# Top-k attention and two gated layers: the second layer's leaky maximum as one parametric relu, and the rounding pass of its weights on another engine

## The chip, the cores and the metric

The kernel runs on one core of one Trainium2 chip. A core has five engines that run side by side, each with a queue of its own that it works through in order: PE (TensorE, matrix products), DVE (VectorE), ACT (ScalarE), POOL (GpSimd) and SP (SyncE, which here only issues transfers). Sixteen DMA engines move data. The metric is device time in microseconds (us) of one execution; lower is better. Times stand as the median of several runs.

## The reference

Three stages follow one another: attention that keeps the 32 largest scores of each row, a layer with a squared relu, and a layer with a leaky maximum. The change touches only the last.

```python
def _attn_ref(q, k, v):                       # 4 batches, 8 heads, 576 rows, 64 wide
    scores = scale * np.matmul(q, k.transpose(0, 1, 3, 2))
    kth = np.partition(scores, -top_k, axis=-1)[..., -top_k:-top_k + 1]
    scores = np.where(scores >= kth, scores, -1000000000.0)
    ...
    return np.matmul(attn, v).astype(np.float32)

def _moe_ref(x, w_in, w_out):                 # x 2304 x 512, w_in 512 x 2048, w_out 2048 x 512
    h = np.maximum(x @ w_in, 0.0)
    return (h * h @ w_out).astype(np.float32)

def _moe2_ref(x, w_in, w_out):
    h = x @ w_in
    g = np.maximum(0.01 * h, h)
    return (g @ w_out).astype(np.float32)
```

## The kernel before, in words

**Precision by splitting.** Products run on numbers rounded to a shorter form. Each operand is therefore kept as two parts: a rounded high part and the remainder. A pass that copies a tile into the rounded form makes the high part, and a subtraction makes the remainder. A product of two split operands is three matmuls: high with high, high with low, low with high.

**Attention.** Scores (L276) are brought out by ACT (L277). DVE then finds the 32 largest of each row with four passes of MAX8 (L828) and three of MATCH_REPLACE8 (L830). ACT masks and exponentiates (L294, a parametric relu; L298), POOL normalizes (L307), PE transposes (L312, L325) and multiplies with the values (L407). The 2304 rows are worked through in 72 pairs of tiles; a "slot" is one sixteenth of a pair, and nearly every step has its slot written in the code.

**The two layers.** The 2304 rows form six blocks of 512, 256, 384, 512, 256 and 384 rows. For each block j and layer there is a phase (j, layer) of 16 steps f, one for each 128 hidden columns. The order of the phases is (0,0) (0,1) (1,0) (1,1) (2,0) (2,1) (3,0) (3,1) (4,0) (5,0) (4,1) (5,1). A step f of `moe` does this:

- 12 matmuls into the PSUM tile `h` (L574), of which there is one buffer (`bufs=1`): the next step's first matmul has to wait until ACT has read it.
- The activation, from `h` into `ga`, then its rounded part `gh` and the remainder `gl` (L600).
- The second product into `acc` for the step before (`LAG = 1`), first with `gh`, then with `gl`: L617 in layer 0, L619 in layer 1. So on PE the order is h(f), acc(f-1), h(f+1), acc(f).

In layer 1 and blocks 0 to 4 the activation is two ACT passes over `h`, one for each sign (L595 into `ga`, L596 into `gb`), and a subtraction on POOL (L597). Then ACT makes `gh` (L599) and POOL `gl`. In block 5 it is an ACT copy scaled by 0.01 (L591) and a maximum on DVE (L592).

**The weights.** They come as 64-bit numbers. In the first phase of each layer, (0,0) and (0,1), `w_convert_steps` turns the two weight tiles of each step (`wi`, `wo`, 128x512) into single precision and splits them: two ACT passes (L508, L509), two DVE passes (L513, L514), one ACT pass for the high part (L518) and a POOL subtraction (L520). It is begun two steps ahead of its use. The result is stored (L528, L529) and loaded again in later phases (L536). `split_hi` is a helper that does the same rounding on ACT (L113) or on POOL (L115), as its third argument says.

**What sets the order.** The pieces of `moe` are emitted between the attention's slots, so many per slot that a group of phases ends about when the next block's rows are ready. A scheduler then sets the order on each engine by priorities and a modelled timeline; at run time each engine's order is fixed.

Of the kernel before, what the change touches and what calls it, by code (L numbers as in the profile page):

```python
# [8 lines left out]
F = mybir.dt.float32  # L9
R = mybir.dt.float32r  # L10
U = mybir.dt.uint32
AF = mybir.ActivationFunctionType
OP = mybir.AluOpType
# [50 lines left out]
KLO_D = ((0, 0), (0, 1))  # L64
QLO_D = (0,)

LEAK2 = 5
GLD = 5


# [1 line left out]
def topk_attention_moe_moe2_kernel(  # L72
# [12 lines left out]
    P = 128  # L85
# [8 lines left out]
    PE, ACT, DVE, POOL, SP = nc.tensor, nc.scalar, nc.vector, nc.gpsimd, nc.sync  # L94
# [6 lines left out]
    def bank():  # L101
        return psum.tile([P, 512], F, tag="att", name="att", bufs=3)
# [4 lines left out]
    def behind(key):  # L107

        return tc.issue_after(cur[key].ins) if key in cur else ExitStack()

    def split_hi(dst, src, act=False):
        if act:
            ACT.activation(dst, src, AF.Copy)  # L113
            return
        POOL.tensor_scalar(dst, src, 1.0, 1.0, op0=OP.mult, op1=OP.mult)  # L115
# [9 lines left out]
    for u in units:  # L125
        for hp in range(NHP):
            n = u["n"]
# [46 lines left out]
    late = {}  # L174
# [197 lines left out]
    def block_x(blk):  # L372

        if "x" not in blk:
            i = SETS[blk["idx"]]
            m = max(x["n"] for x in blocks if SETS[x["idx"]] == i)
            if i == 2:
                ts = [pool.tile([P, 2, m], R, tag="wraw", name="x2", bufs=WRB) for _ in range(NK)]
                blk["x"] = [(t[:, 0], t[:, 1]) for t in ts]
            else:  # L380
                xpool = late["mlp"] if i else pool
                ts = [xpool.tile([P, NK, m], R, tag=f"x{c}{i}", name=f"x{c}{i}", bufs=1) for c in "hl"]
                blk["x"] = [(ts[0][:, c], ts[1][:, c]) for c in range(NK)]
        return blk["x"]
# [76 lines left out]
    steps = [(j, layer, f) for j, layer in phases for f in range(NF)]  # L461
# [8 lines left out]
    def w_alloc(i):  # L470
        wi = pool.tile([P, 2, 512], R, tag="wi", name="wi", bufs=3)
        wo = pool.tile([P, 2, 512], R, tag="wo", name="wo", bufs=4)
        wt[i] = (wi, wo)
        return wi, wo
# [24 lines left out]
    def w_convert_steps(i):  # L499
        if i >= len(steps) or not fresh[i]:  # L500
            return
        w2 = w_alloc(i)
        for raw, w in zip(wraw.pop(i), w2):
            if W64:
                lo, hi = raw[:, :, 0], raw[:, :, 1]
                b = pool.tile([P, 512], U, tag="wc", name="wc", bufs=WCB)
                v = bank()
                ACT.activation(b, lo, AF.Copy, scale=L_SCALE, bias=L_BIAS)  # L508
                ACT.activation(v, hi.bitcast(F), AF.Copy, scale=H_SCALE)  # L509
                yield 0  # L510
                vu, c = v.bitcast(U), b.bitcast(F)
                with behind("dve"):
                    DVE.scalar_tensor_tensor(b, vu, 3, b, op0=OP.logical_shift_left, op1=OP.bitwise_or)  # L513
                DVE.scalar_tensor_tensor(b, vu, 0x80000000, b, op0=OP.bitwise_and, op1=OP.bitwise_or)  # L514
                yield 0
            else:
                c = raw
            ACT.activation(w[:, 0, :], c, AF.Copy)  # L518
            yield 0
            POOL.tensor_tensor(w[:, 1, :], c, w.bitcast(F)[:, 0, :], op=OP.subtract)  # L520
            yield 0
# [30 lines left out]
    def moe(j, layer):  # L552
        blk = blocks[j]
        n = blk["n"]
        x = block_x(blk)
        base = phases.index((j, layer)) * NF
        na = NK if layer == 0 else n // P
        gs = {}
        for f in range(NF + LAG):
            conv = iter(())  # L560
            if f < NF:
                si = base + f
                w_store(si + 1)
                conv = w_convert(si + 2)
                w_load(si + 2)
                wi, wo = wt.pop(si)
                h = late["psum"].tile([P, 512], F, tag="h", name="h", bufs=1)
                cnt = 0
                if f == 0:
                    mm = [(w, c, 0) for w in range(2) for c in range(NK)] + [(0, c, 1) for c in range(NK)]  # L570
                else:
                    mm = [(0, c, y) for c in range(NK) for y in range(2)] + [(1, c, 0) for c in range(NK)]
                for w, c, y in mm:
                    PE.matmul(h[:, 0:n], lhsT=wi[:, w, c * P:(c + 1) * P], rhs=x[c][y][:, 0:n], start=cnt == 0,  # L574
                              stop=cnt == 3 * NK - 1)
                    cnt += 1
                    if cnt % MQ == 0 and cnt < 3 * NK:
                        next(conv, None)
                        yield
                gh = late["mlp"].tile([P, 512], R, tag="gh", name="gh", bufs=2)  # L580
                gl = late["mlp"].tile([P, 512], R, tag="gl", name="gl", bufs=2)
                a = late["mlp"].tile([P, 512], F, tag="ga", name="ga", bufs=2)
                if layer == 0 and j < GLD:
                    ACT.activation(a[:, 0:n], h[:, 0:n], AF.Relu)  # L584
                    ACT.activation(gh[:, 0:n], a[:, 0:n], AF.Square)  # L585
                    POOL.tensor_tensor(a[:, 0:n], a[:, 0:n], a[:, 0:n], op=OP.mult)  # L586
                elif layer == 0:
                    ACT.activation(a[:, 0:n], h[:, 0:n], AF.Relu)
                    ACT.activation(a[:, 0:n], a[:, 0:n], AF.Square)
                elif j >= LEAK2:  # L590
                    ACT.activation(a[:, 0:n], h[:, 0:n], AF.Copy, scale=0.01)  # L591
                    DVE.tensor_tensor(a[:, 0:n], a[:, 0:n], h[:, 0:n], op=OP.max)  # L592
                else:
                    b = late["mlp"].tile([P, 512], F, tag="gb", name="gb", bufs=1)
                    ACT.activation(a[:, 0:n], h[:, 0:n], AF.Relu)  # L595
                    ACT.activation(b[:, 0:n], h[:, 0:n], AF.Relu, scale=-0.01)  # L596
                    POOL.tensor_tensor(a[:, 0:n], a[:, 0:n], b[:, 0:n], op=OP.subtract)  # L597
                if layer or j >= GLD:
                    ACT.activation(gh[:, 0:n], a[:, 0:n], AF.Copy)  # L599
                (DVE if j >= GLD else POOL).tensor_tensor(gl[:, 0:n], a[:, 0:n], gh.bitcast(F)[:, 0:n],  # L600
                                                          op=OP.subtract)
                gs[f] = (gh, gl, wo)
                next(conv, None)
                yield
            if f >= LAG:
                ff = f - LAG
                if ff == 0:
                    acc = [late["psum"].tile([P, 512], F, tag="acc", name="acc", bufs=4) for _ in range(na)]
                gh, gl, wo = gs.pop(ff)
                mm = [(c, w, gh) for c in range(na) for w in range(2)] + [(c, 0, gl) for c in range(na)]  # L610
                if ff == NF - 1:
                    mm.sort(key=lambda m: m[0])
                for i, (c, w, g) in enumerate(mm):
                    cs = slice(c * P, (c + 1) * P)
                    first, last = ff == 0 and g is gh and w == 0, ff == NF - 1 and g is gl
                    if layer == 0:
                        PE.matmul(acc[c][:, 0:n], lhsT=wo[:, w, cs], rhs=g[:, 0:n], start=first, stop=last)  # L617
                    else:
                        PE.matmul(acc[c], lhsT=g[:, cs], rhs=wo[:, w, :], start=first, stop=last)  # L619
                    if i % 3 == 2:  # L620
                        next(conv, None)
                        yield
            for _ in conv:
                pass
            if f < NF:
                w_raw(si + 4)
        for c in range(na):
            if layer == 0:
                xh, xl = x[c]
                ACT.activation(xh[:, 0:n], acc[c][:, 0:n], AF.Copy)  # L630
                DVE.tensor_tensor(xl[:, 0:n], acc[c][:, 0:n], xh.bitcast(F)[:, 0:n], op=OP.subtract)  # L631
            else:
                y = pool.tile([P, 512], F, tag="wc", name="y", bufs=WCB)
                ACT.activation(y, acc[c], AF.Copy)  # L634
                for p0, n0, r0 in rows(blk["g0"] + c * P, P):
                    ACT.dma_start(out[r0:r0 + n0, :], y[p0:p0 + n0])
# [16 lines left out]
    for uh in uhs:  # L653
        b, hp, i = uh["b"], uh["hp"], uh.get("di")
# [158 lines left out]
    while slot <= last:  # L813
        p, i = divmod(slot, 16)
# [89 lines left out]
```

## Time and profile before

| | |
|---|---|
| Median of 3 runs | 1206.67 us (1203.94 to 1209.59) |
| Profiled execution, its own time | 1204.04 us |
| Span of the profiled execution | 1202.3 us |
| Mean granted TensorE clock | 0.979 |
| Busy share of the span: PE, DVE, ACT, POOL | 94%, 79%, 66%, 57% |

The span runs from the first to the last instruction; 1.7 us lie outside it. In the profile the phase (0,0) begins at 173.2 us, (0,1) at 325.4 us, (1,0) at 434.9 us, (4,0) at 963.1 us. These are the starts of the 1st, 193rd, 385th and 1537th matmul of L574. The attention's last MAX8 runs at 962.6 us, so from 963.1 us on the layers are alone.

### The profile page before, as it was taken

What the parts mean: (1) busy time and instruction counts of PE and PEld (TensorE: products, weight loads), DVE (VectorE), ACT (ScalarE), POOL (GpSimd) and SP (SyncE); (2) the same over time, 40 slices, a digit from 0 to 9 for tenths busy, and PEclk for the clock granted to TensorE, in tenths of its full rate; (3) what the DMA queues carried; (4) which work ended last, traced back from release to release, by engine and by line L of the source; (5) the groups of instructions that cost most, each with busy time, mean ns of one, the idle gap of its engine ahead of it and who ended that gap; (6) DMA issues with size and microseconds to landing.
All of it is one profiled execution on the core that took longest, in us unless ns stands there. A gap on an engine that the chain in (4) does not pass through costs nothing.

```text
span 1202.3 us, 20196 instructions
## 1 busy us (share of the span) xinstructions
PE 1133.4 (94%) x6388; PEld 993.1 (83%) x6388; DVE 945.0 (79%) x1944; ACT 798.8 (66%) x1819; POOL 679.4 (57%) x922
## 2 busy tenths in 40 slices
PE   5999967998899999999999999999999999999998
PEld 4777845886677889988998998888788899999997
DVE  7999999768988899999999999999999920110122
ACT  6999978678999986766665666555675653334322
POOL 7967565677889876456665665545456554004200
PEclk9899978898999999999999999999999999999999
DMA  9868556679889888889988888777676689879974
GB/s 302 288 208 264 204 197 210 219 244 347 312 285 339 297 289 289 291 279 398 332 284 294 266 282 289 221 228 225 198 223 225 191 270 374 253 247 351 353 250 137
DMA packets 110522, 323.25 MB, mean 269 GB/s; under 512 B 17488, under 2 KB 25680, under 8 KB 110416
## 3 DMA queue, kind: packets, MB, share of 16 engines
q1 hardware_dynamic: 107776, 317.24, 78.3%
q10 hardware_dynamic: 2640, 4.72, 1.1%
q8 instruction: 52, 0.85, 0.3%
q14 instruction: 54, 0.44, 0.1%
HBM read 254.54 MB, written 67.37 MB: 268 GB/s over the span
## 4 chain that ended last, share of the span: by engine, by line
PE 56%; DVE 4%; ACT 1%; DMA 1%; issue 0%; POOL 0%; SPq 0%; ACTq 0%
PE h L574 24%; PE acc L617 12%; PE acc L619 12%; PE att L407 3%; PE att L312 3%; DVE m L828 2%; DVE w L830 1%; PE att L325 1%; DVE PTs L318 1%; DMA vraw<-in_v_dram 0%; PE att L276 0%; DVE xl L631 0%; ACT y L634 0%; DMA wi<-wd 0%; ACT e L298 0%
## 5 line engine op out<-in xcount | busy, mean ns | idle before, releaser
L574 PE MATMUL h<-xh,wi 128*128 128x512 f32 (+2 forms) x1280 | 349.2, 345 | 14.4 <-ACT gb L596 4.9
L828 DVE MAX8 m<-w 128x8 f32<-128x576 f32 x432 | 312.9, 747 | 1.4
L574 PEld LDWEIGHTS h<-xh,wi 128*128 128x128 f32 x1280 | 227.5, 191 | 41.7 <-ACT gb L596 6.6
L830 DVE MATCH_REPLACE8 w<-m,w 128x576 f32<-128x576 f32 x288 | 213.2, 742 | 0.7
L574 PE MATMUL h<-xl,wi 128*128 128x512 f32 (+2 forms) x640 | 207.3, 342 | 2.3 <-DVE xl L631 1.3
L600 POOL TENSOR_TENSOR gl<-ga,gh 128x512 fp32r<-128x512 f32 (+2 forms) x160 | 163.3, 1021 | 44.6 <-ACT gh L599 40.6
L617 PE MATMUL acc<-gh,wo 128*128 128x512 f32 (+2 forms) x768 | 155.9, 341 | 0.0
L619 PE MATMUL acc<-wo,gh 128*128 128x512 f32 x576 | 152.4, 399 | 1.5 <-ACT gh L599 1.5
L597 POOL TENSOR_TENSOR ga<-ga,gb 128x512 f32<-128x512 f32 (+2 forms) x80 | 81.6, 1020 | 107.9 <-ACT gb L596 106.9
L294 ACT ACTIVATE e<-s,m 128x576 f32<-128x576 f32 x144 | 112.5, 782 | 39.2 <-DVE m L828 32.1
L617 PEld LDWEIGHTS acc<-gh,wo 128*128 128x128 f32 x768 | 126.2, 189 | 10.9 <-ACT gh L585 0.4
L574 PEld LDWEIGHTS h<-xl,wi 128*128 128x128 f32 x640 | 121.2, 191 | 14.8 <-DVE xl L631 3.7
L619 PEld LDWEIGHTS acc<-wo,gh 128*128 128x128 f32 x576 | 103.8, 188 | 21.6 <-ACT gh L599 2.6
L586 POOL TENSOR_TENSOR ga<-ga 128x512 f32<-128x512 f32 (+2 forms) x80 | 66.4, 830 | 84.7 <-ACT gh L585 76.5
L298 ACT ACTIVATE e<-e,nb 128x576 f32<-128x576 f32 x144 | 110.8, 774 | 4.7 <-POOL nb L288 4.4
L828 DVE MAX8 m<-s 128x8 f32<-128x576 f32 x144 | 103.8, 747 | 8.3 <-ACT s L277 5.1
L830 DVE MATCH_REPLACE8 w<-m,s 128x576 f32<-128x576 f32 x144 | 106.9, 743 | 0.4
L312 PE MATMUL att<-ident,e 128*128 128x128 f32 x576 | 88.5, 281 | 18.3 <-ACT e L298 13.9
L584 ACT ACTIVATE ga<-h 128x512 f32<-128x512 f32 (+2 forms) x80 | 39.2, 490 | 85.5 <-PE h L574 77.1
L307 POOL TENSOR_SCALAR e<-e,rc 128x576 f32<-128x576 f32 x108 | 80.0, 753 | 28.2 <-DVE rc L303 26.2
L312 PEld LDWEIGHTS att<-ident,e 128*128 128x128 f32 x576 | 70.2, 144 | 29.9 <-ACT e L298 18.2
L599 ACT ACTIVATE gh<-ga 128x384 fp32r<-128x384 f32 (+2 forms) x112 | 58.4, 522 | 44.7 <-POOL ga L597 34.8
(94 smaller groups left out, 2153.0 us busy)
## 6 DMA issues: line engine op xcount, KB each, us to landing
wi<-wd SPq DMA_DIRECT2D x160, 512.0 KB, 5.0
wo<-wd SPq DMA_DIRECT2D x160, 512.0 KB, 5.1
wraw<-in_w_dram SPq DMA_DIRECT2D x64, 512.0 KB, 5.8
sd<-stage SPq DMA_DIRECT2D x72, 288.0 KB, 3.5
s<-sd SPq DMA_DIRECT2D x72, 288.0 KB, 4.5
wd<-wi SPq DMA_DIRECT2D x32, 512.0 KB, 5.3
wd<-wo SPq DMA_DIRECT2D x32, 512.0 KB, 6.2
kraw<-in_k_dram SPq DMA_DIRECT2D x16, 576.0 KB, 4.5
```

What stands on the lines that cost most here:

```text
L294: ACT.activation(t["e"], t["s"], AF.Prelu, bias=pr["m8"][:, i, 31:32], scale=-1.0, alpha=1.0 / FAR)
L298: ACT.activation(e, e, AF.Exp, bias=pr["nb"][:, i:i + 1], scale=-FAR, accum_out=pr["sum"][:, i:i + 1])
L307: POOL.tensor_scalar(e, e, pr["rc"][:, i:i + 1], 1.0, op0=OP.mult, op1=OP.mult)
L312: PE.transpose(ps[:, j * P:(j + 1) * P], t["e"][:, j * P:(j + 1) * P], ident)
L574: PE.matmul(h[:, 0:n], lhsT=wi[:, w, c * P:(c + 1) * P], rhs=x[c][y][:, 0:n], start=cnt == 0, stop=cnt == 3 * NK - 1)
L586: POOL.tensor_tensor(a[:, 0:n], a[:, 0:n], a[:, 0:n], op=OP.mult)
L597: POOL.tensor_tensor(a[:, 0:n], a[:, 0:n], b[:, 0:n], op=OP.subtract)
L600: (DVE if j >= GLD else POOL).tensor_tensor(gl[:, 0:n], a[:, 0:n], gh.bitcast(F)[:, 0:n], op=OP.subtract)
L617: PE.matmul(acc[c][:, 0:n], lhsT=wo[:, w, cs], rhs=g[:, 0:n], start=first, stop=last)
L619: PE.matmul(acc[c], lhsT=g[:, cs], rhs=wo[:, w, :], start=first, stop=last)
L828: cur["dve"] = DVE.max(out=m8[:, x, 8 * r:8 * r + 8], in_=t["s"] if r == 0 else t["w"])
L830: cur["dve"] = DVE.match_replace(out=t["w"], in_to_replace=m8[:, x, 8 * r:8 * r + 8], in_values=t["s"] if r == 0 else t["w"], imm_value=NEG)
```

## The change

In the second layer (layer 1), all blocks, the activation becomes one ACT pass with a parametric relu, slope 0.01, from `h` into `ga`. The second ACT pass, the tile `gb`, the POOL subtraction, and in block 5 the DVE maximum are gone. The rounding pass of the second layer's weights is done by POOL in place of ACT; those of the first layer stay on ACT. All else in the code stands as before. Lines from L68 on move up by one, from about L590 on by seven.

```diff
-LEAK2 = 5
 GLD = 5
...
                 c = raw
-            ACT.activation(w[:, 0, :], c, AF.Copy)
+            split_hi(w[:, 0, :], c, steps[i][1] == 0)
             yield 0
             POOL.tensor_tensor(w[:, 1, :], c, w.bitcast(F)[:, 0, :], op=OP.subtract)
...
-                elif j >= LEAK2:
-                    ACT.activation(a[:, 0:n], h[:, 0:n], AF.Copy, scale=0.01)
-                    DVE.tensor_tensor(a[:, 0:n], a[:, 0:n], h[:, 0:n], op=OP.max)
                 else:
-                    b = late["mlp"].tile([P, 512], F, tag="gb", name="gb", bufs=1)
-                    ACT.activation(a[:, 0:n], h[:, 0:n], AF.Relu)
-                    ACT.activation(b[:, 0:n], h[:, 0:n], AF.Relu, scale=-0.01)
-                    POOL.tensor_tensor(a[:, 0:n], a[:, 0:n], b[:, 0:n], op=OP.subtract)
+                    ACT.activation(a[:, 0:n], h[:, 0:n], AF.Prelu, alpha=0.01)
                 if layer or j >= GLD:
                     ACT.activation(gh[:, 0:n], a[:, 0:n], AF.Copy)
```

`split_hi` was there already:

```python
    def split_hi(dst, src, act=False):
        if act:
            ACT.activation(dst, src, AF.Copy)
            return
        POOL.tensor_scalar(dst, src, 1.0, 1.0, op0=OP.mult, op1=OP.mult)
```

The scheduler makes a new order on every engine from the first rounding pass of the second layer's weights on, which stands in the last steps of phase (0,0). PE's order is the same up to the first steps of (0,1): its first difference is the 1311th matmul of 6270, where (0,1) begins at the 1309th.

On ACT, this is the order before at the start of phase (0,1); `ga` and `gb` are the two activation passes, L518 the rounding of the weights, L508 their conversion.

```order
L595 ACTIVATE ga<-h 128x512
L596 ACTIVATE gb<-h 128x512
L518 ACTIVATE wi<-wc 128x512
L599 ACTIVATE gh<-ga 128x512
L518 ACTIVATE wo<-wc 128x512
L508 ACTIVATE wc<-wraw 128x512
L595 ACTIVATE ga<-h 128x512
L518 ACTIVATE wi<-wc 128x512
L596 ACTIVATE gb<-h 128x512
```

And this is the same place of the changed kernel, where L590 is the parametric relu, L592 makes `gh`, L507 and L508 are the two passes of the conversion and L316 is the attention's.

```order
L590 ACTIVATE ga<-h 128x512
L592 ACTIVATE gh<-ga 128x512
L590 ACTIVATE ga<-h 128x512
L592 ACTIVATE gh<-ga 128x512
L507 ACTIVATE wc<-wraw 128x512
L316 ACTIVATE PTs<-att 128x4x128
L508 ACTIVATE att<-wraw 128x512
```

The rounding passes and the second read of `h` are gone from between the others, and `gh` follows its `ga` at once.

On POOL, this is the order before in the first steps of (0,1); L597 is the subtraction of the two signs, L520 the remainder of a weight tile, L600 `gl`, L302 and L307 the attention's normalization.

```order
L597 TENSOR_TENSOR ga<-ga,gb 128x512
L520 TENSOR_TENSOR wo<-wc,wo 128x512
L520 TENSOR_TENSOR wi<-wc,wi 128x512
L600 TENSOR_TENSOR gl<-ga,gh 128x512
L302 TENSOR_SCALAR sum<-sum 128x2
L307 TENSOR_SCALAR e_109<-e_109,rc 128x576
L307 TENSOR_SCALAR e_110<-e_110,rc 128x576
L597 TENSOR_TENSOR ga<-ga,gb 128x512
L520 TENSOR_TENSOR wo<-wc,wo 128x512
```

This is the same stretch of the changed kernel; L114 with a weight tile is the rounding pass, L519 the remainder, L593 `gl`, and L114 and L254 with `q` are the attention's.

```order
L114 TENSOR_SCALAR wo<-wc 128x512
L519 TENSOR_TENSOR wo<-wc,wo 128x512
L593 TENSOR_TENSOR gl<-ga,gh 128x512
L114 TENSOR_SCALAR q_83<-qraw 128x320
L114 TENSOR_SCALAR wi<-wc 128x512
L254 TENSOR_TENSOR q_84<-qraw,q_83 128x320
L519 TENSOR_TENSOR wi<-wc,wi 128x512
L114 TENSOR_SCALAR wo<-wc 128x512
L114 TENSOR_SCALAR wi<-wc 128x512
L593 TENSOR_TENSOR gl<-ga,gh 128x512
```

Two rounding passes, whose input comes from DVE, stand where the one subtraction stood, and at some places ahead of `gl`.

## Rows read from the trace of the kernel before

**Rows 1.** The page, parts 1 and 2: busy time by engine; granted clock in 40 slices.

```profile
PE 1133.4 (94%) x6388; PEld 993.1 (83%) x6388; DVE 945.0 (79%) x1944; ACT 798.8 (66%) x1819; POOL 679.4 (57%) x922
...
PEclk9899978898999999999999999999999999999999
```

**Rows 2.** Busy time by stretch: length, then each engine's busy us, clock, DMA.

```profile
core 0: us, PE busy (x) PEld busy (x) DVE busy (x) ACT busy (x) POOL busy (x), PEclk, DMA share, GB/s
0.00:325.40 325.40, 277.05 (x1428) 225.14 (x1428) 289.95 (x599) 272.63 (x668) 229.82 (x322) 0.94 0.75 253
325.40:434.90 109.50, 105.11 (x505) 85.85 (x506) 97.14 (x181) 102.38 (x209) 94.11 (x95) 0.98 0.88 305
434.90:963.10 528.20, 517.82 (x3016) 461.05 (x3015) 521.65 (x1098) 338.30 (x749) 305.11 (x436) 1.00 0.80 266
963.10:1202.30 239.20, 233.47 (x1444) 221.08 (x1443) 36.24 (x69) 85.47 (x195) 50.34 (x72) 1.00 0.81 280
```

**Rows 3.** The chain that ended last, in order of time: start, us, what.

```profile
788.00 2.80 PE h L574 x12
790.81 2.81 PE acc L617 x12
```

**Rows 4.** Waits of PE's weight loads, 325.4 to 434.9 us: total, times, longest.

```profile
PEld h L574 <- ACT gb L596: 3.7, 3, 2.1
PEld h L574 <- ACT xh L630: 2.8, 3, 1.7
PEld att L276 <- DVE wc L514: 1.0, 2, 0.7
PEld acc L619 <- ACT gh L599: 0.9, 1, 0.9
```

**Rows 5.** Waits of DVE, 325.4 to 434.9 us.

```profile
DVE wc L513 <- ACT att L509: 6.2, 7, 1.9
DVE m L828 <- ACT s L277: 3.6, 4, 1.9
```

**Rows 6.** Waits of PE's weight loads, 434.9 to 963.1 us.

```profile
PEld h L574 <- DVE xl L631: 3.7, 5, 1.6
PEld h L574 <- ACT gb L596: 2.9, 2, 1.7
...
PEld acc L619 <- ACT gh L599: 1.2, 2, 0.6
```

**Rows 7.** Groups by line and form, 325.4 to 434.9 us: count, busy us, mean ns.

```profile
L597 POOL TENSOR_TENSOR ga<-ga,gb 128x512 f32<-128x512 f32 x16 | 20.9, 1303 | 2.8 <-ACT gb L596 2.7
...
L518 ACT ACTIVATE wi<-wc 128x512 fp32r<-128x512 f32 x15 | 9.5, 634 | 0.0
L596 ACT ACTIVATE gb<-h 128x512 f32<-128x512 f32 x16 | 9.5, 592 | 0.0
L518 ACT ACTIVATE wo<-wc 128x512 fp32r<-128x512 f32 x15 | 9.5, 631 | 0.0
L595 ACT ACTIVATE ga<-h 128x512 f32<-128x512 f32 x16 | 9.4, 590 | 1.8 <-PE h L574 1.5 <-POOL wo L520 0.2
L599 ACT ACTIVATE gh<-ga 128x512 fp32r<-128x512 f32 x15 | 9.4, 627 | 0.9 <-POOL ga L597 0.9
```

**Rows 8.** Groups by line and form, whole span.

```profile
L294 ACT ACTIVATE e<-s,m 128x576 f32<-128x576 f32 x144 | 112.5, 782 | 39.2 <-DVE m L828 32.1 <-PE att L325 6.6 <-issue 0.3
...
L115 POOL TENSOR_SCALAR q<-qraw 128x320 fp32r<-128x320 f32 x24 | 11.1, 463 | 8.5 <-PE sp L276 7.3 <-PE att L276 0.9
...
L115 POOL TENSOR_SCALAR KTa<-kraw 128x576 fp32r<-128x576 f32 x16 | 10.5, 679 | 1.7 <-DMA kraw<-in_k_dram 1.7
...
L592 DVE TENSOR_TENSOR ga<-ga,h 128x384 f32<-128x384 f32 x16 | 8.9, 554 | 79.6 <-issue 42.9 <-ACT ga L591 36.8
```

**Rows 9.** Timeline, 420 to 424 us: start, us, what, idle before and its releaser.

```profile
419.95 0.57 ACT L595 ACTIVATE ga<-h 128x512 f32<-128x512 f32 x1
...
420.98 0.57 ACT L596 ACTIVATE gb<-h 128x512 f32<-128x512 f32 x1
...
421.60 0.19 PEld L574 LDWEIGHTS h<-xh,wi 128*128 128x128 f32 x1 [1.17 <-ACT gb L596]
```

## The prediction

> **What bounds the kernel now.** The page comes first. PE is busy for 94% of the span and its clock falls only in the early slices [rows 1]. Busy shares are means over unlike stages, so next I cut the span into four stretches and ask in each which engine has no room [rows 2].
>
> - 0 to 325.4 us, up to the end of phase (0,0): PE waits a good deal (277 of 325 us busy). The change has nothing to act on here except one kind of pass in the last steps, and PE's order is the same. I count this stretch as unchanged.
> - 325.4 to 434.9 us, phase (0,1): ACT is busy 102.4 of 109.5 us, PE 105.1, DVE 97.1, POOL 94.1. ACT is nearly full, and here the second layer's weights are converted. PE is not busy for 4.4 us.
> - 434.9 to 963.1 us: DVE, with the attention's maxima, is busy 521.7 of 528.2 us and PE 517.8. PE lacks 10.4 us, DVE only 6.6. ACT (338) and POOL (305) have plenty of room.
> - 963.1 us to the end: PE alone, 233.5 of 239.2 us; the 5.7 us that are missing are the output's last transfer.
>
> A busy PE need not be a PE at its peak, so I check the pace in the chain of work: 12 matmuls of 512 columns take 2.80 us in `h` and 2.81 in `acc` [rows 3]. That is 0.234 us each, and a step of a 512-row block costs 5.6 us. Sixteen steps take 90 of the 109.5 us of (0,1); the attention's 121 other matmuls fill most of the rest. So from 325 us on PE has little to win: at most 4.4 + 10.4 = 14.8 us, 1.2% of the time.
>
> The Trainium skill ("Perfetto Trace Analysis", Identifying the Most-Contended Engine) warns that matmul busy time is a bad measure of distance to the limit, and wants the busy share of the weight loads looked at. By that PE has room in the third stretch (461.1 of 528.2 us, 87%), DVE at 99% is the one bound there, and filling PE's gaps there would be worth nothing. The rows on the pace speak for PE being full as well; the case has its chance as the third case below.
>
> **The change, part by part.**
>
> *Second ACT pass (L596), 80 times in blocks 0 to 4.* In (0,1) 16 of them take 9.5 us [rows 7]. ACT is not the end of any chain outside (0,1), so what counts is when `h` comes free, since PE's next step waits for that pass: 3 waits of 3.7 us in sum in (0,1) [rows 4], 2 of 2.9 us later [rows 6]. A wait does not vanish whole: the first pass still has to read `h`. One of them shows what is saved: the first pass ended at 420.52, the second at 421.55, and PE's weight load, which had waited 1.17 us, went on at 421.60 [rows 7, 9]. Without the second pass 1.03 us go. Where the passes follow each other directly, only the pass itself goes, 0.59 us [rows 7]. For the three in (0,1) I take 1.03 for this one, 0.59 for the longest (2.1), and all of the third (3.7 - 2.1 - 1.2 = 0.4): 2.0 us. For the two later ones, between 0.6 and 1.0 each, 1.5 us in sum.
>
> *Subtraction on POOL (L597), 80 times.* It stands between the two signs and `gh`: 1.30 us [rows 7]. With the second pass, `gh` comes 1.9 us sooner. PE's waits for `gh` are 0.9 us in (0,1) [rows 4] and 1.2 us later [rows 6], the longest 0.9; I let them all go.
>
> *The parametric relu itself.* The trace has no such pass from PSUM with a constant slope. Bounds are a relu from PSUM at the same size, 0.590 us [rows 7], and the attention's parametric relu on 576 columns, 0.782 us [rows 8]. I take 0.59, since source and size are the same there; at 0.78 each release of `h` is 0.2 us later, so five waits give back 1 us.
>
> *Block 5.* The scaled copy becomes a relu of about the same cost, and 16 DVE maxima of 0.554 us [rows 8] go. PE is never short of work there; nothing for the time.
>
> *Rounding on POOL.* ACT loses 30 passes of 0.63 us in (0,1), 19.0 us [rows 7]. With the 9.5 us above ACT goes from 102.4 to 73.9. POOL gets 30 of them. The trace has this operation at 320 columns (0.463 us) and 576 (0.679) [rows 8]; on the line between, 512 columns cost 0.463 + 0.75 x 0.216 = 0.625 us. The upper bound is POOL's two-input pass on the same tile, 1.30 us [rows 7]. I take 0.625: 18.8 us more, against 20.9 us of L597 that go, so POOL stands at 92.0 in place of 94.1. It is no fuller than before, though its passes are now waiting for DVE.
>
> The Trainium skill ("GPSIMD Engine Reference", Engine selection) advises against GpSimd for elementwise work, about 2 times slower than VectorE with two inputs, and about line rate with one. The rounding has one input, and the rows at 320 and 576 columns go with that; read as a rule against any elementwise pass there, it leads to the fifth case below.
>
> *ACT relieved in (0,1).* DVE waits there for the conversion's second ACT pass (L509), 6.2 us, and for scores, 3.6 us [rows 5]. PE feels it as waits for the conversion's scratch bank, 1.0 us [rows 4]; I take half, 0.5 us. What DVE gains beyond this only helps if PE moves too.
>
> *Untouched:* the waits for `xh` and `xl` at a phase's start (2.8 and 3.7 us) [rows 4, 6] belong to layer 0's end.
>
> Sum: (0,1) 2.0 + 0.9 + 0.5 = 3.4 us; later 1.5 + 1.2 = 2.7 us, which DVE's 6.6 us of room allow. Together 6.1 us: 1204.0 - 6.1 = 1197.9 us on the profiled execution's own scale. That execution lies 2.6 us under the median of 1206.7, so as a median 1200.6 us. By 0.5% (6.0 us), about the least that can be told from no change, this is on the edge.
>
> **The cases.**
>
> 1. *The named waits go and little else changes:* 4 to 9 us gained, 1200.6 at the middle. Chance 0.42, half of it beyond 6 us.
> 2. *ACT was what held (0,1):* DVE's waits end, PE closes its 4.4 us there and DVE its 6.6 us later: 11 us, 1195.7. For it speaks ACT at 93%; against it, that PE already keeps its pace. Chance 0.24.
> 3. *DVE holds the time after 434.9 us:* then only (0,1) counts, 3.4 us at most, and a new order can eat that: 1203 to 1207. For it speaks DVE at 99%. Chance 0.22.
> 4. *`gl` waits behind the rounding (slower).* On POOL two rounding passes stand at some places ahead of `gl`, and they wait for DVE's conversion. PE needs `gl(f)` after `h(f+1)` and the 8 `gh` matmuls, 2.8 + 1.9 = 4.7 us after `h(f)`. Prelu, `gh` and `gl` take 0.6 + 0.6 + 1.3 = 2.5, so 2.2 us are spare. If DVE makes POOL wait 4 us in half of the 16 steps, PE loses 8 x 1.8 = 14 us, less the 6 gained: 1215. It decides the sign from 0.4 us lost per step. Against it: in (0,1) DVE itself is freed of ACT. Chance 0.08.
> 5. *The rounding costs as much as a two-input pass, 1.30 us:* POOL needs 94.1 - 20.9 + 30 x 1.30 = 112 us in (0,1). At the 93% that ACT reaches there the phase takes 120 us, 11 more; with the 2.7 us later, 1215. Chance 0.04.
>
> Faster by over 0.5%: 0.22 + 0.24 = 0.46. Same: 0.20 + 0.22 = 0.42. Slower: 0.12. The range leaves out the slower cases and the far end of the second: 1194 to 1209 us. The likeliest case alone has 1197.5 to 1202.5.
>
> **What would show it.** In the profile after: phase (0,1) some 3 us shorter than 109.5; ACT there near 74 us and POOL near 92; no PE wait for `gh`, and waits for `h` that end with the parametric relu, about half as long as those for `gb`; the rounding near 0.62 us on POOL. From 434.9 us on about the same 528 us, less 3; the last 239 us unchanged. I am wrong if (0,1) is longer, with PE waiting for `gl` or for a weight tile from POOL; or if it is shorter by over 6 us, which would mean that ACT's queue held PE by more than PE's own waits name.

## The result, and the profile after

The changed kernel is slower: 1212.9 us median against 1203.2 us, 16 runs each, ratio 1.007 (1.0057 to 1.0083). The forecast was 1200.6 us and a gain. It had been worked out from a median of 1206.7 us over 3 runs; from the 1203.2 us of the 16 runs the same 6.1 us less would have been 1197.1 us.

The profiled execution took 1210.1 us, its span is 1207.9 us. The page's parts 1 and 2, which answer to [rows 1]:

```profile
PE 1133.1 (94%) x6388; PEld 993.6 (82%) x6388; DVE 935.3 (77%) x1928; ACT 756.1 (63%) x1707; POOL 617.4 (51%) x874
...
PEclk9999979899999999999999998999999999999999
```

The work went as the diff says: ACT lost 43 us, POOL 62, DVE 10, and PE has the same 1133 us. So PE stands idle for longer. The busy time by stretch says where; it is cut at the starts of (0,1) (322.7), (1,0) (433.8), (3,0) (729.2) and (4,0) (967.3), and once more after the first steps of (3,0):

```profile
core 0: us, PE busy (x) PEld busy (x) DVE busy (x) ACT busy (x) POOL busy (x), PEclk, DMA share, GB/s
0.00:322.70 322.70, 276.64 (x1427) 224.75 (x1427) 288.87 (x595) 271.27 (x666) 230.11 (x324) 0.94 0.76 254
322.70:433.80 111.10, 106.44 (x512) 86.98 (x511) 97.43 (x184) 80.03 (x161) 93.02 (x112) 0.98 0.86 307
433.80:729.20 295.40, 291.79 (x1920) 275.61 (x1920) 291.46 (x613) 190.76 (x434) 156.50 (x245) 1.00 0.88 305
729.20:755.00 25.80, 14.61 (x63) 11.18 (x62) 25.43 (x56) 12.67 (x26) 6.60 (x12) 0.82 0.56 190
755.00:967.30 212.30, 209.38 (x1027) 173.43 (x1026) 204.54 (x431) 120.02 (x245) 94.47 (x131) 1.00 0.67 212
967.30:1207.90 240.60, 234.28 (x1448) 221.60 (x1446) 27.60 (x53) 81.35 (x180) 36.66 (x53) 1.00 0.80 279
```

The same view of the kernel before, around the start of its phase (3,0) at 739.0 us:

```profile
434.90:739.00 304.10, 297.32 (x1937) 280.24 (x1936) 300.66 (x634) 200.65 (x468) 185.15 (x282) 0.99 0.88 301
739.00:765.00 26.00, 24.54 (x118) 19.32 (x117) 25.70 (x55) 17.42 (x36) 12.59 (x17) 1.00 0.77 247
765.00:963.10 198.10, 195.96 (x965) 161.49 (x964) 195.30 (x411) 120.23 (x247) 107.37 (x137) 1.00 0.68 216
```

At 729.2 us the changed kernel stands where the kernel before stood at 739.0: it is 9.8 us ahead. In the next 26 us PE is busy for 14.6 us in place of 24.5, its clock is at half for part of it, and the lead is gone. DVE is full on both sides of that place, before and after (25.4 of 25.8 us, 25.7 of 26.0).

How much of the lead is time that the change won? The stretch from the start of (0,1) to that of (3,0), first before, then changed:

```profile
325.40:739.00 413.60, 402.43 (x2440) 366.09 (x2441) 397.80 (x814) 303.02 (x676) 279.25 (x376) 0.99 0.88 302
322.80:729.20 406.40, 398.13 (x2429) 362.55 (x2429) 388.79 (x797) 270.69 (x592) 249.42 (x357) 1.00 0.87 306
```

Of the 9.8 us, 2.6 come from ahead of (0,1), where single profiles differ by as much anyway (last section). PE's idle time fell from 11.2 to 8.3 us: 2.9 us are what fewer waits gave. The other 4.3 us are less busy time: 11 matmuls of the attention stand behind the start of block 3 in the new order (2429 in place of 2440), and less of the stretch ran at the lower clock (mean 1.00 in place of 0.99); this comes back as busy time later. So the change won 2.9 us up to here, and lost 9.7 us in the 26 us that follow (11.2 us without PE work in place of 1.5). From there to the end PE is idle for 1.4 us more than before. With the 2.6 us this is the whole of the 5.6 us between the two spans.

The timeline of the changed kernel there, on PE, DVE and ACT (start, us, what, idle before and its releaser). L573 is the first product, L412 and L427 bring block 3's last rows from the attention into `xh`, L293 and L297 are the attention's masking and exponential, L583 is the first read of `h`:

```profile
729.21 0.86 PE L573 MATMUL h<-xh,wi 128*128 128x512 f32 x3
...
734.35 0.41 PE L324 MATMUL att<-ident,e 128*64 128x128 f32 x2 [1.20 <-DVE xf L412]
...
741.62 0.43 DVE L412 TENSOR_TENSOR xf<-att,tmp 64x256 f32<-64x256 f32 x1
...
742.08 0.42 ACT L427 ACTIVATE xh<-xf 128x256 fp32r<-128x256 f32 x1 [2.24 <-DVE xf L412]
...
742.55 2.50 PE L573 MATMUL h<-xh,wi 128*128 128x512 f32 x5 [4.69 <-ACT xh L427]
...
746.90 0.48 PE L573 MATMUL h<-xl,wi 128*128 128x512 f32 x1
...
747.83 0.78 ACT L293 ACTIVATE e<-s,m 128x576 f32<-128x576 f32 x1 [0.70 <-DVE m L821]
...
750.76 0.58 ACT L583 ACTIVATE ga<-h 128x512 f32<-128x512 f32 x1
...
751.40 0.50 PE L573 MATMUL h<-xh,wi 128*128 128x512 f32 x1 [4.02 <-ACT ga L583]
```

The same place of the kernel before:

```profile
743.23 0.43 DVE L413 TENSOR_TENSOR xf<-att,tmp 64x256 f32<-64x256 f32 x1
...
744.78 0.42 ACT L428 ACTIVATE xh<-xf 128x256 fp32r<-128x256 f32 x1 [0.52 <-DVE w L830]
...
745.25 1.43 PE L574 MATMUL h<-xh,wi 128*128 128x512 f32 x5 [0.21 <-ACT xh L428]
...
748.31 0.51 PE L574 MATMUL h<-xh,wi 128*128 128x512 f32 x1 [0.69 <-ACT ga L584]
```

Two things are to be seen. First, block 3's last rows are ready at nearly the same time in both, 741.6 and 743.2 us, because DVE makes them and has lost and won little. PE comes 10 us sooner, multiplies the three of four column parts of the block that are there (128 of 512 columns each), does what is left of block 2 and of the attention, and waits 4.7 us for the last part. Second, the read of `h` comes late. PE's last matmul into `h` starts at 746.9, but ACT works in order, and ahead of the read stand a masking pass that waits 0.7 us for DVE's maximum (L293, 747.8), two exponentials, and two copies of the attention's transposed weights (L316, L333). The read starts at 750.8, and PE loses another 4.0 us. The second step begins at 751.4 us, in the kernel before at 748.3: 9.8 us ahead has become 3.1 us behind.

How early PE comes can be counted: DVE's MAX8 that have started before (3,0) starts, first the kernel before (L828), then the changed one (L821). Length, DVE busy us of these and their count, clock, DMA:

```profile
0.00:739.00 739.00, 306.35 (x428) 0.97 0.83 280
0.00:729.20 729.20, 301.57 (x423) 0.97 0.82 283
```

Block 3's last rows stand behind 432 MAX8 in DVE's order before and behind 431 in the changed kernel.

### The profile page after: what moved, and what is told of

The parts are those of the page before. It is cut to its first block, busy times and chain, and to the rows that moved or that the text cites. A ratio compares the mean times of both kernels' runs of the same rounds, so it can differ in the third digit from the quotient of the medians.

```text
span 1207.9 us, 20017 instructions
## 1 busy us (share of the span) xinstructions
PE 1133.1 (94%) x6388; PEld 993.6 (82%) x6388; DVE 935.3 (77%) x1928; ACT 756.1 (63%) x1707; POOL 617.4 (51%) x874
## 4 chain that ended last, share of the span: by engine, by line
PE 57%; DVE 3%; ACT 2%; issue 0%; ACTq 0%; DMA 0%; POOL 0%; DVEq 0%
PE h L573 25%; PE acc L612 13%; PE acc L610 12%; PE att L406 4%; PE att L311 3%; DVE m L821 1%; DVE w L823 1%; PE att L324 1%; PE att L275 1%; ACT e L297 1%; ACT y L627 0%; DVE PTs L317 0%; DVE xl L624 0%; ACT e L293 0%; DMA wi<-wd 0%
## 5 line engine op out<-in xcount | busy, mean ns | idle before, releaser
L573 PE MATMUL h<-xh,wi 128*128 128x512 f32 (+2 forms) x1280 | 352.1, 347 | 22.8 <-ACT ga L583 6.2
L821 DVE MAX8 m<-w 128x8 f32<-128x576 f32 x432 | 313.2, 747 | 1.2
L573 PEld LDWEIGHTS h<-xh,wi 128*128 128x128 f32 x1280 | 228.0, 191 | 49.7 <-ACT ga L583 7.4
L593 POOL TENSOR_TENSOR gl<-ga,gh 128x512 fp32r<-128x512 f32 (+2 forms) x160 | 162.7, 1017 | 165.6 <-ACT gh L592 125.8
L573 PE MATMUL h<-xl,wi 128*128 128x512 f32 (+2 forms) x640 | 209.2, 344 | 1.8 <-DVE xl L624 1.6
L593 DVE TENSOR_TENSOR gl<-ga,gh 128x384 fp32r<-128x384 f32 x32 | 17.9, 559 | 150.7 <-ACT gh L592 148.9
L573 PEld LDWEIGHTS h<-xl,wi 128*128 128x128 f32 x640 | 122.2, 192 | 14.9 <-DVE xl L624 4.0
L293 ACT ACTIVATE e<-s,m 128x576 f32<-128x576 f32 x144 | 112.4, 780 | 35.3 <-DVE m L821 30.8
L590 ACT ACTIVATE ga<-h 128x512 f32<-128x512 f32 (+2 forms) x96 | 46.9, 488 | 134.7 <-PE h L573 133.3
L297 ACT ACTIVATE e<-e,nb 128x576 f32<-128x576 f32 x144 | 110.9, 774 | 4.9 <-POOL nb L287 4.7
L821 DVE MAX8 m<-s 128x8 f32<-128x576 f32 x144 | 104.1, 747 | 7.5 <-ACT s L276 5.4
L316 ACT ACTIVATE PTs<-att 128x512 fp32r<-128x512 f32 x108 | 62.1, 597 | 42.2 <-PE att L311 41.5
```

Of the source, the lines that this page charges most:

```text
L293: ACT.activation(t["e"], t["s"], AF.Prelu, bias=pr["m8"][:, i, 31:32], scale=-1.0, alpha=1.0 / FAR)
L297: ACT.activation(e, e, AF.Exp, bias=pr["nb"][:, i:i + 1], scale=-FAR, accum_out=pr["sum"][:, i:i + 1])
L316: ACT.activation(pts[:, 0:4, c:c + P], x, AF.Copy)
L821: cur["dve"] = DVE.max(out=m8[:, x, 8 * r:8 * r + 8], in_=t["s"] if r == 0 else t["w"])
```

## The experiments

Three theories of the loss. **A**: DVE holds the time from about 435 us on; a faster PE comes early to block 3's rows and gives the gain back there. **B**: the rounding on POOL costs, since it waits for DVE ahead of `gl` and the weights. **C**: any new order costs or gains some us by chance. Ratios are to runs of the kernel before on the same chip.

**The parametric relu alone** (the rounding stays on ACT).

```diff
-            split_hi(w[:, 0, :], c, steps[i][1] == 0)
+            ACT.activation(w[:, 0, :], c, AF.Copy)
```

> Only the activation is changed (one parametric relu); the second layer's weights are rounded on ACT as before. Theory A (DVE holds the time from 435 us on: PE gets ahead because its waits are gone, then has no work until block 3's rows are ready, and gives it back there): (3,0) is again some 125 to 130 us long with stalls of 8 us or more at its start, and the time is no better than before, 1203 to 1213 us. Theory B (the rounding on POOL is what costs, by waiting for DVE in front of gl and the weights' remainders): without it the waits for gb and gh are simply won, 1195 to 1199 us. Theory C (any new order of instructions costs or gains some us by chance): no statement on the sign; phases other than (3,0) should then differ as well.

1211.9 us, ratio 1.0054 (1.0033 to 1.0075): the loss is there without the rounding, which speaks against B. Phase (3,0) is 123.2 us long (112.8 before) and again begins after 423 MAX8. Waits of PE's weight loads, 735 to 760 us:

```profile
PEld att L406 <- DVE PTs L334: 1.5, 1, 1.5
PEld att L311 <- POOL e L306: 1.5, 1, 1.5
PEld att L324 <- DVE xf L412: 1.3, 1, 1.3
PEld att L406 <- ACT e L293: 1.2, 1, 1.2
PEld h L573 <- ACT ga L583: 1.1, 1, 1.1
PEld att L406 <- DVE PTs L317: 1.1, 1, 1.1
PEld acc L610 <- ACT gh L584: 0.4, 1, 0.4
```

Busy time from (0,1) to (3,0), and in the first 26 us of (3,0):

```profile
325.80:738.10 412.30, 400.99 (x2429) 364.26 (x2429) 390.87 (x798) 283.86 (x622) 231.85 (x328) 0.99 0.87 301
738.10:764.00 25.90, 19.75 (x86) 15.20 (x85) 25.44 (x55) 14.14 (x29) 7.99 (x13) 0.87 0.62 199
```

PE lacks 6.2 us in those 26 (1.5 in the kernel before), now on one piece of the attention's chain after another. The read of `h` is late by 1.1 us only, as it was before, so that second stall is no necessary part.

But A holds only by half here. PE is no earlier in time: (3,0) begins at 738.1 us, in the kernel before at 738.9, and PE lacked 11.3 us on the way, before 11.2. DVE is late: it is idle for 21.4 us on the way in place of 15.8, and block 3's last rows are made at 750.5 us in place of 743.2. What this run shares with the changed kernel is a place in PE's order: the same 11 matmuls fewer stand ahead of block 3 (2429). Other phases differ as well ((1,0) is 76.4 us in place of 72.7), which is what C expected.

**The rounding on POOL alone** (the activation as before).

```diff
-            ACT.activation(w[:, 0, :], c, AF.Copy)
+            split_hi(w[:, 0, :], c, steps[i][1] == 0)
```

> Only the rounding pass of the second layer's weights goes to POOL; the two-pass leaky maximum stays. Theory A: POOL gets 20 us more in (0,1) and is then its fullest engine, so (0,1) may grow by up to 6 us, but block 3 starts without long stalls (under 4 us); 1201 to 1208 us. Theory B: (0,1) longer by the whole of the changed kernel's loss, 1209 to 1216 us. Theory C: anything between.

1205.4 us, ratio 1.0007 (0.9994 to 1.0021). Its phase (0,1):

```profile
322.10:443.00 120.90, 113.02 (x531) 91.24 (x530) 109.30 (x208) 92.66 (x190) 116.10 (x137) 0.96 0.82 289
```

POOL is full there (116.1 of 120.9 us) and the phase 11 us longer, which went beyond the 6 us expected; but more of the attention's matmuls are done in it (531 PE matmuls in place of 505), block 3 begins after 428 MAX8 without long stalls, and the whole kernel is as fast as before. Here a longer phase made no longer kernel while DVE went on. B falls.

**Both kernels with DVE's maxima over half a row** (288 of 576 columns; the selection leaves out the other half).

```diff
-                cur["dve"] = DVE.max(out=m8[:, x, 8 * r:8 * r + 8], in_=t["s"] if r == 0 else t["w"])
+                src = (t["s"] if r == 0 else t["w"])[:, 0:S // 2]
+                cur["dve"] = DVE.max(out=m8[:, x, 8 * r:8 * r + 8], in_=src)
...
-                cur["dve"] = DVE.match_replace(out=t["w"], in_to_replace=m8[:, x, 8 * r:8 * r + 8],
-                                               in_values=t["s"] if r == 0 else t["w"], imm_value=NEG)
+                src = (t["s"] if r == 0 else t["w"])[:, 0:S // 2]
+                cur["dve"] = DVE.match_replace(out=t["w"][:, 0:S // 2], in_to_replace=m8[:, x, 8 * r:8 * r + 8],
+                                               in_values=src, imm_value=NEG)
```

> The kernel before with DVE's maxima and replacements over the first 288 of 576 columns of each score row, so that the selection is made over half a row; nothing else is left out. DVE's 1008 passes fall from about 0.745 to 0.45 us, some 300 us less, so DVE can't hold the time any more. All theories: faster than before. It is the partner of the next run. Theory A: here PE alone sets the pace from 325 us on.

> The changed kernel with the same shortened DVE passes (selection over half a row). Theory A: with DVE out of the way the change is worth what PE's waits for gb and gh were, so it is faster than its partner by 3 to 12 us, and no stall of over 4 us stands at block 3's start. Theory B: it is slower than its partner by about as much as the changed kernel was than the kernel before, 5 to 12 us. Theory C: within 5 us either way.

1193.9 us (0.9905, 0.9887 to 0.9922) and 1189.3 us (0.9867, 0.9849 to 0.9884). With DVE out of the way the change gains 4.6 us, and no wait of PE is listed between 735 and 760 us in either. The same relief is worth some 9 us to the kernel before (1203.2 - 1193.9) and some 24 us to the changed one (1212.9 - 1189.3, runs of different chips): DVE holds the changed kernel far more.

**DVE relieved in full work.** For every second attention tile from the fourth unit on (54 tiles), ACT copies the transposed tile to SBUF and POOL makes the remainder that DVE made.

```diff
-            DVE.tensor_tensor(pts[:, 4:8, c:c + P], x, pts.bitcast(F)[:, 0:4, c:c + P], op=OP.subtract)
+            if t["i"] % 2 == 1:
+                xs = late["pool"].tile([P, 4, P], F, tag="xs", name="xs", bufs=1)
+                ACT.activation(xs, x, AF.Copy)
+                POOL.tensor_tensor(pts[:, 4:8, c:c + P], xs, pts.bitcast(F)[:, 0:4, c:c + P], op=OP.subtract)
+            else:
+                DVE.tensor_tensor(pts[:, 4:8, c:c + P], x, pts.bitcast(F)[:, 0:4, c:c + P], op=OP.subtract)
```

> The changed kernel, and for every second attention tile from the fourth unit on (54 of 108) the remainder of the transposed weights (0.68 us on DVE, reading PSUM) is made without DVE: ACT copies the bank to SBUF (some 0.6 us), POOL subtracts (1.3 us). The result is the reference's. DVE loses some 36 us, most of it between 435 and 960 us; ACT and POOL get 32 and 70 us where each has 40% of its time free. Theory A: DVE comes to block 3's rows sooner, the stalls at its start fall under 5 us, and the change's gain is seen: 1188 to 1200 us, faster than before. Theory C (it was only an unlucky order): another order, another time, 1198 to 1215 us, with stalls at some other place.

> The same relief of DVE on the kernel before (two-pass leaky maximum, rounding on ACT). Theory A: worth less than on the changed kernel, since DVE held it less, and ACT and POOL, which stay loaded by the old activation, take the passes in (0,1) worse: 1196 to 1206 us, slower than the previous run by 3 to 12 us. Theory C: the two differ either way.

On the changed kernel 1191.4 us, ratio 0.9883 (0.9865 to 0.9902); on the kernel before 1198.7 us, 0.9949 (0.9933 to 0.9965). The change that costs 0.7% by itself gains 0.6% (1191.4 / 1198.7) once DVE is rid of 54 passes of 0.68 us (its busy time falls from 935 to 903 us). Waits of PE's weight loads on the changed kernel with the relief, 725 to 760 us, all that are listed:

```profile
PEld att L311 <- POOL e L306: 1.9, 2, 1.6
PEld h L578 <- ACT xh L432: 0.2, 1, 0.2
```

And its busy time in (0,1) and up to (4,0):

```profile
326.20:431.70 105.50, 103.62 (x506) 85.24 (x506) 92.97 (x175) 81.57 (x165) 100.94 (x119) 1.00 0.90 326
431.70:949.90 518.20, 511.67 (x3010) 457.61 (x3009) 496.12 (x1058) 343.95 (x754) 311.79 (x432) 1.00 0.78 269
```

Block 3 begins at 730.7 us, about as early as in the changed kernel (729.2), but by then 435 MAX8 have started, and PE waits only 0.2 us for the rows. This is the fastest version with the full selection.

**The parametric relu alone, with the same relief.** Its diff is the first experiment's and the one above.

> Parametric relu in the second layer, its weights rounded on ACT, and DVE relieved of every second remainder. Theory A: the parametric relu alone is worth most of what the whole change is worth with DVE relieved; the rounding counts only in (0,1): 1191 to 1197 us, between the kernel with both (1191.4) and the relieved kernel before (1198.7). Theory B: faster than 1190.

1198.2 us, ratio 0.9933 (0.9907 to 0.9959): no better than the relieved kernel before, and beyond the 1191 to 1197 us that A had expected. This is a miss for A: with DVE relieved the parametric relu alone should have been worth most of the gain. Its phases from (1,0) on are within 1 us of those of the run with both parts, but (0,1) is 113.8 us in place of 105.5. So of the gain with both parts most lies in (0,1), where the rounding is what differs. Whether it is the rounding's cost on ACT or the order that comes with it stays open: the last run below rounds on POOL too, and its (0,1) takes 112.2 us.

**The parametric relu from block 3 on alone.**

```diff
-                elif j >= LEAK2:
-                    ACT.activation(a[:, 0:n], h[:, 0:n], AF.Copy, scale=0.01)
-                    DVE.tensor_tensor(a[:, 0:n], a[:, 0:n], h[:, 0:n], op=OP.max)
+                elif j >= 3:
+                    ACT.activation(a[:, 0:n], h[:, 0:n], AF.Prelu, alpha=0.01)
```

> The parametric relu from block 3 on alone (blocks 0 to 2 keep the two passes), rounding on ACT. Its order is that of the kernel before up to the second layer of block 3, so PE can't come early to block 3. Theory A: no loss at block 3's start, and little to win after, since PE and DVE are both full there: 1200 to 1206 us, within 0.3% of before. Theory B says the same, as nothing is rounded on POOL. A theory that the parametric relu itself is slow on ACT would have phases (3,1) to (5,1) longer by 1 us or more each.

1205.7 us, ratio 1.0003 (0.9986 to 1.0019). Where the code up to block 3 is the old one (428 MAX8 at its start), the parametric relu neither costs nor gains.

**The read of `h` ahead.** On the changed kernel, block 3's first read of `h` is issued on ACT before the masking passes that follow it in the program.

```diff
-        ACT.activation(t["e"], t["s"], AF.Prelu, bias=pr["m8"][:, i, 31:32], scale=-1.0, alpha=1.0 / FAR)
+        with behind("ga"):
+            ACT.activation(t["e"], t["s"], AF.Prelu, bias=pr["m8"][:, i, 31:32], scale=-1.0, alpha=1.0 / FAR)
...
-                    ACT.activation(a[:, 0:n], h[:, 0:n], AF.Relu)
+                    ga = ACT.activation(a[:, 0:n], h[:, 0:n], AF.Relu)
+                    if j == 3 and f == 0:
+                        cur["ga"] = ga
```

> The changed kernel, with ACT's first read of h of block 3 set ahead of two masking passes (and the two exponentials behind them) that wait for DVE's maxima; PE's order up to there is the changed kernel's. Theory A: PE comes just as early and stalls just as long for block 3's rows (about 5 us), but the second stall, 4.3 us for the read of h, falls to about 1 us: 1207 to 1210 us, so 3 to 6 us of the loss were ACT's order and the rest is PE's early coming. If the read were late for another reason, the stall stays and the time is 1211 to 1215 us.

1206.0 us, ratio 1.000 (0.9983 to 1.0017): the whole loss is won back, more than the 3 to 6 us that were expected. Waits of PE's weight loads, 725 to 760 us:

```profile
PEld h L574 <- ACT xh L428: 4.9, 1, 4.9
...
PEld h L574 <- ACT ga L584: 1.2, 1, 1.2
```

The wait for the rows is as long as ever, the wait for the read fell from 4.3 to 1.2 us. In the two profiled executions, from the start of (3,0) on, this is worth 4 us (474.7 us in place of 478.7); the medians differ by more, and where the rest lies the traces don't tell. What is left fits theory A without the late read: what PE is ahead at block 3 it gives back there, and the sum is nothing.

**More relief, and later relief.** DVE relieved of all 108 remainders (with two buffers for the copies), and of every second one only from tile 48 on (48 tiles, not 46). The lines that differ from the relief above, one version after the other:

```diff
-            if t["i"] % 2 == 1:
-                xs = late["pool"].tile([P, 4, P], F, tag="xs", name="xs", bufs=1)
+            if True:
+                xs = late["pool"].tile([P, 4, P], F, tag="xs", name="xs", bufs=2)
...
-            if t["i"] % 2 == 1:
+            if t["i"] % 2 == 1 and t["i"] >= 48:
```

> The changed kernel with the remainder of the transposed weights made by ACT and POOL for all 108 attention tiles from the fourth unit on (in the run before, for 54). DVE loses 73 us, ACT gets 65, POOL 140. Theory A: DVE is out of the way and PE alone is left; its stalls after 325 us were some 20 us at most, so the second half of the relief brings little: 1184 to 1192 us. If POOL (then some 63% of the span, and full in (0,1)) takes DVE's place: 1192 to 1205 us.

> The changed kernel with DVE relieved of every second remainder only from tile 48 on (46 tiles), that is from about phase (0,1) on, so that ACT and POOL stay free of it in phase (0,0). DVE loses some 31 us, less than with 54 tiles (37), nearly all of it after 325 us. Theory A: what counts is that block 3's rows are ready when PE comes; the stalls at its start stay under 4 us, and (0,0) is about 150 us as in the changed kernel in place of 154: 1187 to 1193 us. If the relief in (0,0) was needed to bring DVE forward, stalls of 5 us or more come back at block 3: 1193 to 1205 us.

1208.8 us (1.0027, 1.0006 to 1.0047) and 1194.0 us (0.9896, 0.9878 to 0.9914). The second lies 1 us beyond A's range; the stalls are gone as A expected (PE lacks 0.9 us in the first 26 us of (3,0)), but it is not faster than relief from the start. The first is a miss. DVE is far ahead there (461 MAX8 at the start of (3,0)), no stall stands at block 3, but (0,0) takes 159 us in place of 150 and (2,0) 92 in place of 83. POOL in (0,1) has 100.7 of 106.2 us, as with half the relief, and in (2,0) DVE is as full as ever:

```profile
577.00:669.00 92.00, 87.28 (x542) 85.37 (x541) 91.11 (x197) 66.83 (x145) 78.83 (x104) 0.98 0.87 304
```

So the second half of the relief costs more than it brings; by which wait wasn't settled.

**What this leaves of the theories.** B is out. For A speak the pairs with DVE relieved, in which the stalls at block 3 go and the change gains, and the read ahead, with which the loss goes. But among the versions without relief the stalls and PE's order go together: the changed kernel, the parametric relu alone and the read ahead have the attention's 11 matmuls behind the start of block 3, come there after 423 MAX8 and stall; the kernel before, the rounding alone and the parametric relu from block 3 on have them ahead of it, come after 428 MAX8, and have no wait of over 2.1 us there. Whether PE's won time or the scheduler's new order alone, as C has it, brings PE there before its rows was not tested apart. A run of the changed activation in the old order would tell.

## Why the prediction was wrong

**What held.** The prices: the parametric relu from PSUM takes 0.592 us on 512 columns (0.59 taken), the rounding on POOL 0.625 and 0.624 us (0.625 taken). The two groups in the changed kernel:

```profile
L590 ACT ACTIVATE ga<-h 128x512 f32<-128x512 f32 x32 | 18.9, 592 | 25.9 <-PE h L573 25.7
...
L114 POOL TENSOR_SCALAR wi<-wc 128x512 fp32r<-128x512 f32 x16 | 10.0, 624 | 6.5 <-DVE wc L513 5.7 <-DVE rc L302 0.6
```

ACT in (0,1) came down from 102.4 to 80.0 us, less far than to the 74 forecast; POOL stands at 93.0 (92). No wait for `gh` is left in the list of (0,1). From 434 to 729 us PE lacks 3.6 us in place of 6.8 from 435 to 739 before: 3.2 us less, where the sum's second part had 2.7.

**What failed first: (0,1).** Its 3.4 us did not come: 111.1 us in place of 109.5, with 7 more matmuls, and PE lacks 4.7 us in place of 4.4. Waits of PE's weight loads there, against [rows 4]:

```profile
PEld h L573 <- POOL wo L519: 2.7, 2, 1.8
PEld h L573 <- issue: 1.8, 1, 1.8
PEld h L573 <- DVE xl L624: 1.2, 2, 0.8
```

The waits for `gb` went, and others of the same size took their place; POOL's rounding now waits 5.7 us for DVE's conversion (row above), as the fourth case had it, but far less than it needed. In the pair with DVE's passes over half a row the phase takes 107.5 us with the old activation and 104.4 with the change: the 3 us are there when DVE doesn't hold them. In the pair with every second remainder moved the phase takes 108.9 us and 105.5 with the change, and the rest up to the end 760.8 and 758.6: 3.4 and 2.2 us, close to the forecast's 3.4 and 2.7. Two other versions with relief and the parametric relu have 113.8 and 112.2 us in (0,1), so some of that closeness may be luck.

**What failed in the end: the step "Sum".** It added PE's waits up and took them off the end, with DVE's 6.6 us of room as the only limit. It took the order of the rest as given. But room counted over 528 us is not room at one place. The time of block 3's last rows hangs on DVE (741.6 us, 743.2 before); in the new order PE is there 9.8 us sooner, its queue has nothing else to do, and it loses 9.7 us more than before in the first 26 us of (3,0), against 2.9 us of waits won ahead of it. The third case named the right engine and still gave 0 to 3 us; it took it that a PE held by DVE loses nothing. One part of that surplus is shown: the late read of `h`, without which the change is neutral. For the parametric relu alone, where that read is not late and PE not early, the loss lies at the same place, in PE's waits on the attention's chain, and DVE's 5.6 us of further idle time ahead of it; why DVE waits more there was not taken apart. So the place and DVE's part in it are shown; what brings PE there ahead of its rows stays open, as said above.

The sentence of the Trainium skill that judges PE by its weight loads ("Perfetto Trace Analysis", Identifying the Most-Contended Engine) would have made the third stretch worth nothing. The runs go with it: with DVE's work as it was, no version beat the kernel before; with less of it, all but one did.

The slower cases of the prediction were not it. Waits of `gl` on POOL cost PE 0.4 us in all from 434 to 729 us, and the rounding has its low price.

## What to carry to other kernels

Where two engines are both nearly full, ask where one waits for the other next: a wait taken from the engine that is not the last one can come back at the next place where it needs the other's result. Take work off the engine that sets that place first (here 54 passes of 0.68 us on DVE, at the price of a copy on ACT and a subtraction on POOL), and only then shorten the other's path; here the same change then gained 0.6% where it had cost 0.7%. When a scheduler makes a new order, count what has moved across such a place before a lead is put down to waits saved. And look at what stands ahead, in an in-order queue, of a short step that frees a single buffer: with the passes there set behind it, PE's wait fell by 3 us.

## What the runs showed that was not expected

PE's clock fell while PE waited for the rows. Granted clock of the changed kernel in two pieces of 5 us at that place, by stretch:

```profile
740.00:745.00 5.00, 2.45 (x6) 1.96 (x7) 4.94 (x13) 1.02 (x2) 2.29 (x4) 0.50 0.34 134
...
750.00:755.00 5.00, 3.60 (x10) 2.87 (x11) 4.93 (x11) 1.98 (x5) 2.83 (x4) 0.74 0.41 153
```

PE was busy 1.8 of the 5 us before the first. At 752.4 us the clock went to its lower level (0.5 of full, 1.2 GHz) once more, for 3.4 us (the mean is 0.74 from 750 to 755 us and 0.92 from 755 to 760), after the second stall had ended: matmuls that follow each other without a wait came every 0.43 us there in place of 0.23, which by these figures costs some 1.6 us on top of the stalls (an estimate).

Phase (0,0) has nearly the same order in the seven versions with full selection and no relief ahead of tile 48, and took 148.2 to 152.7 us in them; so differences of 2 to 4 us between single profiles say nothing by themselves.
